# Gated attention and SwiGLU mix on one core: two gate-factor loads issued earlier, the first attention quad's fills dealt 4, 3, 3, and the last two PSUM banks swapped before some long visits

## The chip, the cores and the metric

One core of a Trainium2 chip runs the whole program in one launch. The metric is the device time of a launch in microseconds, and the number reported is the median over several launches. Beside it stands one launch that the hardware profiler recorded; its span runs from the first instruction to the last.

Engines are named as in the profile: PE multiplies matrices into PSUM, which has eight banks of 128 x 512 fp32; DVE, ACT and POOL work on vectors; SP issues DMA transfers, as ACT and POOL do too.

## The reference, cut to what matters

```python
x = A_x                                            # 1 x 2048 x 640
g = sigmoid((x * gate_w).sum(-1, keepdims=True))   # one gate factor per row
a = attention(x, wq, wk, wv, wo, beta)             # 32 heads of 20, 4 segments of 512
b = (silu(x @ w1) * (x @ w3)) @ w2                 # hidden width 1728
return g * a + (1 - g) * b
# attention, for each segment s of 512 rows and each head:
#   a_dot = softmax(q k^T * 20**-0.5 + causal mask) v
#   a_mem = phi(q) M / (phi(q) z + 1e-6)           # M, z from the segments before
#   o = sigmoid(beta) * a_mem + (1 - sigmoid(beta)) * a_dot
#   M += phi(k)^T v ; z += sum phi(k)
# the heads' outputs are joined and multiplied by wo
```

## The kernel before, in words

**Tiling.** The 2048 rows are four chunks of 512, one for each segment. Activations lie transposed, 128 features on the partitions and the 512 rows of a chunk along the free axis. Dense products split both operands into a high and a low part and make three passes (high by high, high by low, low by high). One output block of 128 x 512 that sums over 640 features is 15 matmuls into one PSUM bank.

**Dense work.** Q, K and V projections, the feed-forward network (`ffn_up` makes tiles named g and u, `ffn_down` makes tiles named f), the read of the memory from earlier segments (`memory_read`, tiles nd) and the output projection (`oproj`, tiles op) are generators. A generator yields after each few matmuls with an estimate of the PE time it has just laid down. Chunks 0 and 1 are group A, chunks 2 and 3 group B. The generators are strung together by hand into units; the list `segs` says up to which point of the attention each unit lasts.

**Attention.** The 128 pairs of a chunk and a head go through in 32 quads, four heads of one chunk at a time. Each quad owns 40 slots. At slot 5 (`BIG`) comes a long visit of PE to the attention, at slot 17 (`SMALL`) a short one. A visit deals fills from a table, `VISITS`: an `s` fill makes logits for the row maxima (two banks; DVE reduces them, L641), a `t` fill makes transposed logits of the quad before (two banks; ACT takes the exponential, L673), and `o` is the product with V (one bank; DVE copies it out, L691). A long visit has eight entries and takes 15 banks' worth of tiles, a short one three. For quad number m = 1 there is no `o` yet, and its long visit is split in two, at slots 5 and 11 (L800). Before a visit of fewer than four entries the dense work may stop in the middle of a block ("amid"); before one of four or more it runs on until no block is open ("between").

**Banks.** `bank_tile` (L111) takes PSUM banks round robin: it pops the first of the list `free`. A tile that is filled at once puts its bank at the end of the list straight away. A dense block that stays open for a while is `held`, and its bank goes to the end when the block is full (`filled`). Whoever writes a bank next must wait until the last reader of its old content is done.

**What sets the order.** PE's instructions stay in the order in which the program was written. The other engines' streams are laid out by a scheduler at build time, except for instructions marked `here`, which keep their place. All engines run their streams in order, so an instruction that waits holds up all that stands behind it on its engine.

**Gate factors.** The first row of `ed` in DRAM has, for each row of a chunk, the factor that the sum of both branches is multiplied by at the end. `load_share` (L738) broadcasts 512 of them to all 128 partitions, in a DMA issued from ACT's queue and marked `here`; the tile is called sh. `share` (L541) multiplies a finished output block by it: L543, on DVE, or on POOL for chunk 2 and the even blocks of chunk 1. Chunk 0's factors are loaded at the start of chunk 0's last down projection (L569), chunk 1's at the start of its output projection proper, behind the normalization (L831). Chunk 3 has a buffer of its own; chunks 0, 1 and 2 share one.

**Normalization.** `normalize` (L753) runs before a chunk's output projection, one block of 128 features at a time. A matmul spreads the softmax denominators (tile rr), and DVE multiplies the attention's output by them (L762). For chunks after the first, four transposes bring the memory's part (tile gt, L766), DVE adds it (L767), ACT rounds the sum to its high part (L768) and DVE takes the low part (L769). These blocks are braided into the up projections of a feed-forward unit, so PE works on a g or u block between them.

Of the kernel before, what the change touches and what calls it, by code (L numbers as in the profile page):

```python
# [25 lines left out]
BIG = -1.0e38  # L26
# [12 lines left out]
def gated_mix(ctx: ExitStack, tc: tile.TileContext, xT, wqk, wv, w13, w2, w2h, wo, beta, out):  # L39
# [63 lines left out]
    last = {}  # L103
# [5 lines left out]
    free, held = list(range(NB)), {}  # L109

    def bank_tile(name, hold=None):  # L111


        k = free.pop(0)
        ps = pp.tile([P, L], F32, tag=f"b{k}", name=name, bufs=1)
        if hold:
            held[k] = -hold
        else:
            free.append(k)
        return ps  # L120
# [443 lines left out]
    def ffn_down(cs, js, idx, last=()):  # L564
        first = js[0] == 0
        w2s = [w_get(i, idx[0]) for i in idx]
        for c in cs:
            if c in last and c < 2:
                load_share(c)  # L569
            if first:  # L570
                accs[c] = slot(f"acc{c}")[:, :KB * L].rearrange("p (b n) -> p b n", b=KB)
            for fb in range(KB):
                for n0, n1 in ((0, 256), (256, L)) if last and (c, fb) == (NSEG - 1, KB - 1) else ((0, L),):
                    ps = bank_tile(f"f{c}_{js[0]}_{fb}_{n0}", 1300 if len(js) > 2 else 690)
                    ms = []
                    for j, w in zip(js, w2s):
                        for a, b in (PASSES if j < NF else ((0, 0), (0, 1))):
                            ms.append((w[:, b, fb * P:(fb + 1) * P], hts[c, j][:, a, n0:n1]))
                    for n, (w, h) in enumerate(ms):
                        nc.tensor.matmul(ps[:, :n1 - n0], w, h, start=n == 0, stop=n == len(ms) - 1)  # L580
                        if n % 3 == 2 and n < len(ms) - 1:
                            yield 699.0 if n == 2 and len(ms) > 5 else 699
                    filled()
                    dst = accs[c][:, fb]
                    if first:
                        nc.scalar.copy(dst, ps)
                    elif c not in last:
                        nc.vector.tensor_add(dst, ps, dst)  # L588
                    elif c < 2:
                        finish(c, fb, ps)  # L590
                    else:
                        finish_shared(c, fb, ps, n0, n1 - n0)
                    yield 699 if len(ms) % 3 == 0 else 466

    def both_shares():
        for c in B:
            load_share(c)
            yield 1

# [153 lines left out]
    def normalize(c):  # L753

        assert c in turned
        if not c:
            gms[c] = big_tile(f"oT{c}", FR)[:, :KB * L].rearrange("p (b n) -> p b n", b=KB)
        for b in range(KB):
            o, hi = f_tile(f"on{c}_{b}"), gms[c][:, b]
            ps = bank_tile(f"rr{c}_{b}")  # L760
            nc.tensor.matmul(ps, sel[:, b * P:(b + 1) * P], rR, start=True, stop=True)
            nc.vector.tensor_mul(o, oall[c][:, b].bitcast(F32), ps)  # L762
            if c:
                pt = bank_tile(f"gt{c}_{b}")
                for qb in range(4):
                    nc.tensor.transpose(pt[:, qb * P:(qb + 1) * P], hi[:, qb * P:(qb + 1) * P].bitcast(F32), ident)  # L766
                nc.vector.tensor_add(o, o, pt)  # L767
            nc.scalar.copy(hi, o)  # L768
            nc.vector.tensor_sub(oall[c][:, b], o, hi.bitcast(F32))  # L769
            yield 700  # L770
# [22 lines left out]
    def attention():  # L793

        for m in range(-1, NQUAD + 2):
            for n in range(40):
                if m == -1 and n < 40 - LEAD:
                    continue

                todo = VISITS.get(n, ()) if m != 1 else {BIG: VISITS[BIG][:3], BIG + 6: VISITS[BIG][4:]}.get(n, VISITS.get(n, ()))  # L800
                todo = [(kind, m - q, f) for kind, q, *f in todo if 0 <= m - q < NQUAD]
                if todo:
                    yield "amid" if len(todo) < 4 else "between"
# [16 lines left out]
    def oproj(c, plan):  # L820

        ws, oT = [], []

        def first():
            yield from normalize(c)
            oT.extend((gms[c], oall[c]))

        def rest():
            ws.extend(w_get(i, plan[0]) for i in plan)
            if c == 1:  # L830
                load_share(c)  # L831
            for fb in range(KB):
                ps = bank_tile(f"op{c}_{fb}", 1300)
                n = 0
# [52 lines left out]
    def chain(jobs):  # L887
        return sum(c for c, _ in jobs), (y for _, g in jobs for y in g)
# [41 lines left out]
    seg = [d, braid(chain(u), o1, 5), o2] + [job_up(A, j) for j in GROUPS[3][2:]] + [job_down(A, 3)]  # L930
    u0, u1 = jobs_up_by_chunk(A, 4)
    x2, x3 = split_x(2), split_x(3)
    seg += [(0, load_raw(2)), (0, load_raw(3))] + u0 + [braid(chain(u1), (0, x2), 4, 0, False)]
    d = job_down(A, 4, (0,))
    q = job_q(B[:1], 0, {2: big_tile})
    seg += [braid(chain([braid(d, (0, x2), 5)] + q), (0, x3), 4, 10)] + job_v(B)
# [21 lines left out]
    segs.append((NJ + LAG, seg))  # L958
    d, u = job_down(B, 3), jobs_up(B, 4)
    o1, o2 = jobs_oproj(3)  # L960
    tail = [braid(chain([d, (0, both_shares())] + u), o1, 4, 10)] + [braid(o2, (0, shared(2)), 3), job_down(B, 4, B)]

    for n, (_, g) in enumerate(head):
        for _ in g:
# [29 lines left out]
    while run:  # L994
# [7 lines left out]
        if isinstance(place, str):  # L1002

            for _ in range(4 if place == "amid" else 8):
                if (max(held.values(), default=-1) >= 0) if place == "amid" else not held:
                    break
                d = step(run)
                if d is None:
                    break
                credit -= d  # L1010
            next(att)
        slots += 1
        credit += run[2]
# [66 lines left out]
```

## Time and profile before

| | |
|---|---|
| median of 3 launches | 1105.04 us (1104.69 to 1105.52) |
| the profiled launch | 1107.25 us |
| its span, first to last instruction | 1105.4 us |
| between that span and that launch's time | 1.85 us |
| the profiled launch above the median | 2.21 us |
| DVE busy | 598.1 us (54%) |
| POOL busy | 584.6 us (53%) |
| ACT busy | 381.3 us (34%) |

How to read it: a row of the timeline has the start in us from the start of the span, the time from the first of its instructions to the end of the last, engine, line, operation, written tile, read tiles, shape, and count. In brackets stands how long the engine was idle before it, and who released it. Matmuls are pipelined, so a 128 x 512 matmul is recorded for some 0.4 us though a new one starts every 0.23 us. A wait of PE therefore shows in brackets only as far as it outlasts the matmul before it; the whole of it is read from start times.

### The profile page before, as it was taken

Reading aid. Unit: us, or ns where it says so; the run is one execution under the profiler, and the core shown is the slowest. Engines: PE = TensorE matmul, PEld = TensorE weight load, DVE = VectorE, ACT = ScalarE, POOL = GpSimd, SP = SyncE. Lnnn points to the kernel's source line nnn. Section 1 sums busy time; section 2 is a strip of 40 time slices with the busy share of each in tenths; the row PEclk is TensorE's granted clock in tenths of the full one; section 3 lists DMA queues with packets and bytes.
Section 4 is the critical chain, followed back from the end, with each engine's and each line's share of the span. In section 5 each row is a group of like instructions: output and inputs, shape, how many; then the busy total and the mean of one; then the engine's idle time right before and its main releaser. Section 6 shows DMA issues by size and latency. Waiting matters only on the chain.

```text
span 1105.4 us, 17904 instructions
## 1 busy us (share of the span) xinstructions
PE 1094.9 (99%) x6290; PEld 853.0 (77%) x6290; DVE 598.1 (54%) x1711; ACT 381.3 (34%) x826; POOL 584.6 (53%) x729
## 2 busy tenths in 40 slices
PE   9999999999999999999999999999999999999998
PEld 6988877777777777787977777777777777777787
DVE  5032564356555554366153678875557665651575
ACT  6244233343233122145244543325333332223020
POOL 5055556366366363565066447556774665655263
PEclk9999999999999999999999999999999999999999
DMA  8256943334355134435367966365664343433122
GB/s 306 110 205 220 281 125 82 95 82 116 77 142 129 51 84 123 126 94 171 121 197 265 288 215 183 97 161 146 151 159 109 85 116 96 117 103 89 52 79 95
DMA packets 87545, 153.20 MB, mean 139 GB/s; under 512 B 11584, under 2 KB 25184, under 8 KB 87456
## 3 DMA queue, kind: packets, MB, share of 16 engines
q1 hardware_dynamic: 63040, 106.30, 30.1%
q0 software_dynamic: 20384, 38.68, 15.9%
q10 hardware_dynamic: 4032, 7.08, 1.8%
q8 instruction: 50, 0.82, 0.3%
q14 instruction: 39, 0.32, 0.1%
HBM read 96.56 MB, written 54.54 MB: 137 GB/s over the span
## 4 chain that ended last, share of the span: by engine, by line
PE 93%; DVE 4%; ACT 1%; DMA 1%; issue 1%; ACTq 0%; SPq 0%; DVEq 0%
PE g L257 16%; PE f L580 16%; PE u L257 16%; PE k L257 6%; PE v L385 6%; PE op L837 6%; PE o L687 6%; PE q L257 5%; PE s L634 5%; PE t L667 4%; PE nd L352 1%; PE pm L449 1%; PE q L327 1%; DVE junk L641 1%; DMA sh<-ed 1%
## 5 line engine op out<-in xcount | busy, mean ns | idle before, releaser
L641 DVE CUSTOM_DVE_ANT_0 junk<-s,mask 128x256 bf16<-128x256 f32 (+3 forms) x512 | 250.3, 489 | 105.9 <-PE s L634 73.6
L673 ACT ACTIVATE P<-t 128x512 f32<-128x512 f32 (+1 forms) x384 | 172.5, 536 | 190.2 <-PE t L667 153.0
L257 PE MATMUL g<-X,W 128*128 128x512 f32 x840 | 208.5, 398 | 0.0
L179 POOL TENSOR_TENSOR W<-wr,W 128x640 fp32r<-128x640 f32 (+1 forms) x126 | 198.5, 1581 | 2.5
L174 POOL CAST W<-wr 128x640 fp32r<-128x640 f32 (+1 forms) x126 | 92.5, 739 | 202.0 <-PE f L580 47.7
L580 PE MATMUL f<-ht,W 128*128 128x512 f32 (+1 forms) x825 | 197.0, 395 | 0.7 <-DVE acc L550 0.7
L257 PE MATMUL u<-X,W 128*128 128x512 f32 x780 | 196.7, 399 | 0.0
L677 POOL TENSOR_SCALAR_AFFINE_SELECT P<-P 128x256 f32<-128x256 f32 x192 | 94.6, 502 | 183.2 <-ACT P L673 182.9
L257 PEld LDWEIGHTS g<-X,W 128*128 128x128 f32 x840 | 155.9, 188 | 36.6 <-issue 0.4
L580 PEld LDWEIGHTS f<-ht,W 128*128 128x128 f32 x825 | 152.9, 188 | 37.6 <-DVE acc L550 1.5
L257 PEld LDWEIGHTS u<-X,W 128*128 128x128 f32 x780 | 144.0, 188 | 34.4 <-ACT P L673 0.3
L107 POOL TENSOR_TENSOR ht<-ft,ht 128x512 fp32r<-128x512 f32 x52 | 67.2, 1291 | 90.1 <-ACT ht L106 90.0
L611 POOL DMA_DIRECT2D qk<-qkd x128 | 83.6, 655 | 0.5 <-issue 0.2
L634 PE MATMUL s<-qk 60*128 60x256 f32 (+3 forms) x512 | 77.8, 345 | 1.1 <-DVE fu L520 1.0
L257 PE MATMUL k<-X,W 128*128 128x512 f32 x300 | 77.0, 403 | 0.0
L687 PE MATMUL o<-P,vg 128*32 128x512 f32 (+3 forms) x1024 | 75.5, 435 | 1.4 <-DVE on L767 1.4
L519 ACT ACTIVATE ft<-g 128x512 f32<-128x512 f32 x52 | 31.2, 599 | 124.9 <-PE g L257 113.8
L385 PE MATMUL v<-W,X 128*128 128x320 f32 (+1 forms) x480 | 71.9, 311 | 0.3 <-ACT P L673 0.3
L520 DVE SCALAR_TENSOR_TENSOR fu<-ft,g 128x512 f32<-128x512 f32 x52 | 35.7, 686 | 67.3 <-ACT ft L519 58.3
L385 PEld LDWEIGHTS v<-W,X 128*128 128x128 f32 x480 | 71.0, 189 | 1.0 <-ACT P L673 0.5
L106 ACT CAST ht<-ft 128x512 fp32r<-128x512 f32 x52 | 32.2, 619 | 110.9 <-DVE ft L528 110.8
L588 DVE TENSOR_TENSOR acc<-f,acc 128x512 f32<-128x512 f32 x65 | 44.7, 689 | 44.8 <-PE f L580 44.6
(123 smaller groups left out, 1204.8 us busy)
## 6 DMA issues: line engine op xcount, KB each, us to landing
qk<-qkd POOLq DMA_DIRECT2D x128, 240.0 KB, 4.0
wr<-in_w_dram SPq DMA_DIRECT2D x80, 320.0 KB
qkd<-qs SPq DMA_DIRECT2D x20, 512.0 KB
qkd<-ks SPq DMA_DIRECT2D x20, 512.0 KB
od<-oq SPq DMA_DIRECT2D x32, 256.0 KB
wr<-in_wo_dram SPq DMA_DIRECT2D x20, 320.0 KB
vg<-vd SPq DMA_DIRECT2D x16, 336.0 KB
xr<-in_xT_dram SPq DMA_DIRECT2D x20, 256.0 KB
```

The costliest lines, as they stand in the source:

```text
L107: (lo or nc.gpsimd.tensor_sub)(dst[:, 1], src, dst[:, 0].bitcast(F32))
L174: hi = nc.gpsimd.tensor_copy(w[:, 0, :n], raw[:, :n])
L179: last["low"] = nc.gpsimd.tensor_sub(w[:, 1, :n], raw[:, :n], w[:, 0, :n].bitcast(F32))
L257: nc.tensor.matmul(ps, w[:, a, kb * P:(kb + 1) * P], x[:, b, kb, :], start=n == 0, stop=n == 14)
L385: nc.tensor.matmul(ps[:, :n1 - n0], x[:, a, kb, lb * P:(lb + 1) * P], wvt[kb][:, b, n0:n1], start=n == 0, stop=n == 14)
L580: nc.tensor.matmul(ps[:, :n1 - n0], w, h, start=n == 0, stop=n == len(ms) - 1)
L611: here(nc.gpsimd.dma_start(t[64 * i:64 * i + RH], qkd[c][RH * (h + i):RH * (h + i + 1)]))
L634: nc.tensor.matmul(ps[i][:, o:o + w], q[:, qb * P:(qb + 1) * P], key[:, :w], start=n == 0, stop=n == len(todo) - 1, skip_group_check=True)
L641: nc.vector.tensor_tensor_reduce(out=junk[:, :w], in0=ps[i][:, o:o + w], in1=mask[:, L - w:], scale=1.0, scalar=-3.0e38, op0=ALU.add, op1= ...
L673: last["exp"] = nc.scalar.activation(pairs[2 * m + k]["P"][:, i, o:o + n], ps[i][:, b:b + n], AF.Exp, scale=SCALE)
L677: nc.gpsimd.affine_select(d, d, pattern=[[0, 2], [0, n], [1, P]], base=0, channel_multiplier=-1, compare_op=ALU.is_ge, fill=0.0)
L687: nc.tensor.matmul(ps[32 * i:32 * i + 32, kb * P:], heads[2 * p + i]["v"][:, kb], pairs[p + i // 2]["P"][:, i % 2, o:o + n], start=kb == 0 ...
```

## The change

Three edits that don't depend on each other.

1. **Loads of gate factors.** Chunk 0's load leaves `ffn_down` and is put among the loads of the raw inputs of chunks 2 and 3, ahead of the up projections of the last feed-forward group of chunks 0 and 1. Chunk 1's load moves from behind its normalization to ahead of it. The helper for chunks 2 and 3 takes a list and does what it did.
2. **First quad.** For m = 1 the long visit at slot 5 takes four fills in place of three (t fill 3 joins), and the one at slot 11 three in place of four. The short visit keeps three. With four, the first visit is now one of those before which no dense block stays open, and the second is one that may cut a block.
3. **Swap.** The last `held` dense tile's first letter and the bank of the last gt tile are remembered. Before a long visit, if the last but one bank in the list is that gt bank and the last dense tile was a u, f or o(p) block, the last two entries of the list change places.

```diff
@@ bank_tile
         if hold:
             held[k] = -hold
+            last["dense"] = name[0]
@@ ffn_down
         for c in cs:
-            if c in last and c < 2:
-                load_share(c)
             if first:
@@
-    def both_shares():
-        for c in B:
+    def load_shares(cs):
+        for c in cs:
             load_share(c)
             yield 1
@@ normalize
                 pt = bank_tile(f"gt{c}_{b}")
+                last["gt"] = free[-1]
@@ attention
-                todo = VISITS.get(n, ()) if m != 1 else {BIG: VISITS[BIG][:3], BIG + 6: VISITS[BIG][4:]}.get(n, VISITS.get(n, ()))
+                todo = VISITS.get(n, ()) if m != 1 else {BIG: VISITS[BIG][:3] + VISITS[BIG][4:5], BIG + 6: VISITS[BIG][5:]}.get(n, VISITS.get(n, ()))
@@ oproj
         def first():
+            if c == 1:
+                load_share(c)
             yield from normalize(c)
@@
         def rest():
             ws.extend(w_get(i, plan[0]) for i in plan)
-            if c == 1:
-                load_share(c)
@@ the units
-    seg += [(0, load_raw(2)), (0, load_raw(3))] + u0 + [braid(chain(u1), (0, x2), 4, 0, False)]
+    seg += [(0, load_raw(2)), (0, load_raw(3)), (0, load_shares(A[:1]))] + u0 + [braid(chain(u1), (0, x2), 4, 0, False)]
...
-    tail = [braid(chain([d, (0, both_shares())] + u), o1, 4, 10)] + [braid(o2, (0, shared(2)), 3), job_down(B, 4, B)]
+    tail = [braid(chain([d, (0, load_shares(B))] + u), o1, 4, 10)] + [braid(o2, (0, shared(2)), 3), job_down(B, 4, B)]
@@ the loop over slots, before a visit
+            if place == "between" and free[-2] == last.get("gt") and last["dense"] in "ufo":
+                free[-2:] = free[:-3:-1]
             next(att)
```

In the rows that follow, a name's first digits are chunk, quad or block, and its last number is only a serial number. Line numbers are those of each kernel.

**PE in the first quad.** Before, from the last matmuls of the memory read nd1_2_0 (chunk 1) to the second visit:

```order
L634 MATMUL s1_0_1_1476<-qk1_91 128x512
L667 MATMUL t0_0_0_1483<-qk0_90 128x512
L667 MATMUL t0_1_1_1492<-qk0_90 128x128
L257 MATMUL u1_0_1438<-X1_105,W16_989 128x512 x3
L257 MATMUL g0_1_1507<-X0_103,W17_1075 128x512 x6
L352 MATMUL nd1_2_1_1520<-Ms0_4_1145,pq1_271 128x147
L257 MATMUL g0_1_1507<-X0_103,W17_1075 128x512 x9
L667 MATMUL t0_3_0_1543<-qk0_90 128x512
L634 MATMUL s1_2_0_1551<-qk1_91 128x512
L634 MATMUL s1_1_1_1571<-qk1_91 128x128
L352 MATMUL nd1_3_0_1589<-Ms0_0_714,pq1_271 128x147
```

Now:

```order
L258 MATMUL u1_0_1438<-X1_105,W16_989 128x512 x3
L633 MATMUL s1_0_1_1483<-qk1_91 128x512
L666 MATMUL t0_1_1_1499<-qk0_90 128x128
L666 MATMUL t0_3_1_1508<-qk0_90 128x512
L258 MATMUL g0_1_1515<-X0_103,W17_1075 128x512 x6
L353 MATMUL nd1_2_1_1528<-Ms0_4_1145,pq1_271 128x147
L633 MATMUL s1_2_0_1536<-qk1_91 128x512
L633 MATMUL s1_1_1_1556<-qk1_91 128x128
L258 MATMUL g0_1_1515<-X0_103,W17_1075 128x512 x9
L353 MATMUL nd1_3_0_1589<-Ms0_0_714,pq1_271 128x147
```

The last three matmuls of u1_0 moved ahead of the first visit, t0_3 from the second visit to the first, and the second visit now cuts the open block g0_1 after six of its matmuls in place of following it. The matmuls are the same. With the round robin this changes which old content each tile waits for: g0_1 now takes the bank of s1_0_0 (before, that of nd1_2_0), t0_3_1 that of u1_0, and s1_1_1 that of t0_3_1 (before, that of g0_1).

**DVE at chunk 0's last down projection.** f0_13_n and f1_13_n are its output blocks of chunks 0 and 1, X2 and X3 the low parts of the inputs of chunks 2 and 3. Before:

```order
L550 TENSOR_TENSOR acc0_1953<-f0_13_1_0_5020,acc0_1953 128x512
L132 TENSOR_TENSOR X2_4932<-xr2_4776,xh2_3_5038 128x512
L550 TENSOR_TENSOR acc0_1953<-f0_13_2_0_5029,acc0_1953 128x512
L543 TENSOR_TENSOR acc0_1953<-acc0_1953,sh0_4999 128x512 x2
L550 TENSOR_TENSOR acc0_1953<-f0_13_3_0_5047,acc0_1953 128x512
L132 TENSOR_TENSOR X2_4932<-xr2_4776,xh2_4_5065 128x512
L543 TENSOR_TENSOR acc0_1953<-acc0_1953,sh0_4999 128x512
L550 TENSOR_TENSOR acc0_1953<-f0_13_4_0_5056,acc0_1953 128x512
```

Now:

```order
L551 TENSOR_TENSOR acc0_1953<-f0_13_1_0_5020,acc0_1953 128x512
L544 TENSOR_TENSOR acc0_1953<-acc0_1953,sh0_4790 128x512 x2
L133 TENSOR_TENSOR X2_4934<-xr2_4776,xh2_3_5038 128x512
L551 TENSOR_TENSOR acc0_1953<-f0_13_2_0_5029,acc0_1953 128x512
L133 TENSOR_TENSOR X2_4934<-xr2_4776,xh2_4_5065 128x512
L551 TENSOR_TENSOR acc0_1953<-f0_13_3_0_5047,acc0_1953 128x512
L551 TENSOR_TENSOR acc0_1953<-f0_13_4_0_5056,acc0_1953 128x512
L544 TENSOR_TENSOR acc0_1953<-acc0_1953,sh0_4790 128x512
```

The first two multiplications by the gate factors stand right behind the add of block 1 in place of block 2. From there to the add of the last block, f1_13_4, DVE has 19 instructions in both kernels. On ACT, the load of sh0 stands directly behind the last exponential of the visit before the g blocks, some twenty instructions earlier than it did; on SP, the store of the first finished block now stands ahead of one weight load.

**ACT and DVE at the normalization of chunk 1.** on1_b is the block being normalized, u2_2 the dense block around it, s19, t18 and o34 the fills of the visit that follows. ACT before:

```order
L655 DMA qk0_90<-mr_7222 2x8x128 x2
L768 CAST gm1_6764<-on1_0_7250 128x512
L519 ACTIVATE ft2_2_7269<-g2_2_7233 128x512
L768 CAST gm1_6764<-on1_1_7277 128x512
L673 ACTIVATE P36_7326<-t18_0_0_7324 128x512
L106 CAST ht2_2_7268<-ft2_2_7269 128x512
```

ACT now:

```order
L654 DMA qk0_90<-mr_7222 2x8x128 x2
L739 DMA sh1_7250<-ed1_85 128x512
L768 CAST gm1_6764<-on1_0_7252 128x512
L520 ACTIVATE ft2_2_7271<-g2_2_7233 128x512
L768 CAST gm1_6764<-on1_1_7279 128x512
L672 ACTIVATE P36_7328<-t18_0_0_7326 128x512
```

DVE before:

```order
L762 TENSOR_TENSOR on1_1_7277<-oall1_6264,rr1_1_7278 128x512
L767 TENSOR_TENSOR on1_1_7277<-on1_1_7277,gt1_1_7281 128x512
L762 TENSOR_TENSOR on1_2_7298<-oall1_6264,rr1_2_7299 128x512
L528 SCALAR_TENSOR_TENSOR ft2_2_7269<-fu2_2_7270,u2_2_7273 128x512
L641 ISA junk_7320,m76_7138<-s19_0_0_7316,mask_89 128x512
L767 TENSOR_TENSOR on1_2_7298<-on1_2_7298,gt1_2_7302 128x512
L769 TENSOR_TENSOR oall1_6264<-on1_1_7277,gm1_6764 128x512
```

DVE now:

```order
L761 TENSOR_TENSOR on1_1_7279<-oall1_6264,rr1_1_7280 128x512
L761 TENSOR_TENSOR on1_2_7300<-oall1_6264,rr1_2_7301 128x512
L767 TENSOR_TENSOR on1_1_7279<-on1_1_7279,gt1_1_7283 128x512
L767 TENSOR_TENSOR on1_2_7300<-on1_2_7300,gt1_2_7304 128x512
L529 SCALAR_TENSOR_TENSOR ft2_2_7271<-fu2_2_7272,u2_2_7275 128x512
L640 ISA junk_7322,m76_7138<-s19_0_0_7318,mask_89 128x512
L769 TENSOR_TENSOR oall1_6264<-on1_1_7279,gm1_6764 128x512
```

The load of chunk 1's factors now stands ahead of the cast of on1_0. The add of gt1_2 moved from behind the first reduction of s19 to ahead of the read of u2_2. Swapped are the banks that o34 and t18_3_0 take: o34 now follows u2_2, t18_3_0 follows gt1_2. The rule fires at one more visit, some 65 us later and without a normalization beside it: there o40 takes the bank of f3_0_1 and t21_3_0 that of f3_0_0, the other way round than before. No other tile changes the content that it waits for, but for those of the first quad.

## The prediction

> **What bounds the kernel now.** I read the page first, then PE's waits, then the timelines around the waits. On the page:
>
> ```profile
> PE 1094.9 (99%) x6290; PEld 853.0 (77%) x6290; DVE 598.1 (54%) x1711; ACT 381.3 (34%) x826; POOL 584.6 (53%) x729
> PE 93%; DVE 4%; ACT 1%; DMA 1%; issue 1%; ACTq 0%; SPq 0%; DVEq 0%
> ```
>
> PE is the bound nearly everywhere: it is busy for 99% of the span and holds 93% of the chain that ended last. All that can be won without fewer matmuls is where PE waits. One long stretch of the chain gives PE's pace, and the list of PE's waits the longest ones:
>
> ```profile
> 354.61 21.00 PE f L580 x90
> ...
> PE o L687 <- DVE on L767: 1.4, 1, 1.4
> PE s L634 <- DVE fu L520: 1.0, 1, 1.0
> PE f L580 <- DVE acc L550: 0.7, 2, 0.4
> ```
>
> A 128 x 512 matmul every 0.233 us; and but for the start of the program no wait exceeds 1.4 us. The three edits go one to each of these rows. So some 5 us, 0.45%, is the most that can come of it, and the question is how much of each wait is replaced by another. I call the three places A (first quad), B (chunk 0's last down projection) and C (normalization of chunk 1).
>
> **A: the first quad.** PE, DVE and ACT there:
>
> ```profile
> 145.60 0.85 PE L352 MATMUL nd<-Ms,pq 128*128 128x147 f32 x6
> 146.38 0.50 PE L634 MATMUL s<-qk 60*128 60x512 f32 x2
> 147.27 0.97 PE L257 MATMUL u<-X,W 128*128 128x512 f32 x3
> 148.22 1.64 PE L257 MATMUL g<-X,W 128*128 128x512 f32 x6
> 153.41 0.33 PE L634 MATMUL s<-qk 60*128 60x384 f32 x1
> 154.72 0.50 PE L634 MATMUL s<-qk 60*128 60x384 f32 x3 [0.98 <-DVE fu L520]
> ...
> 146.69 0.25 DVE L358 RECIPROCAL nd_r<-nd_r 128x16 f32<-128x16 f32 x1
> 147.52 0.55 DVE L359 SCALAR_TENSOR_TENSOR gm<-nd,gate,nd_r 128x320 f32<-128x320 f32 x1
> 148.59 0.68 DVE L528 SCALAR_TENSOR_TENSOR ft<-fu,u 128x512 f32<-128x512 f32 x1
> ...
> 147.14 2.07 ACT L673 ACTIVATE P<-t 128x512 f32<-128x512 f32 x4 [4.01 <-PE t L667]
> ```
>
> The last s fill wants the bank of g0_1, whose matmuls end just ahead of the visit; ACT and DVE have yet to read it. The two halves of the fill start 1.31 apart, of which 0.98 is idle; I count 1.1 as wait. Before that, three u matmuls take 0.95 in place of 0.70; 0.1 of it is the change from the visit's small tiles, so 0.14 is wait. **Removed: 1.24.**
>
> What comes in: g0_1 now takes s1_0_0's bank. The three u matmuls go first, so the visit starts at 146.38 + 0.70 = 147.08. Its first three fills took 0.89 (146.38 to 147.27), t0_3 another 0.34 (the s pair of 512 columns in B's rows, 512.34 to 512.68), and g0_1 could start at 148.31. DVE is free at 146.94, and in its new order makes gm (0.55), ft1_0 (0.68) and then the reduction of s1_0_0 (0.69 for this size); each starts some 0.07 before the one ahead ends, so the bank is free at 146.95 + 0.48 + 0.61 + 0.69 = 148.73, and g0_1 starts near 148.8. **Added: 0.49.** The second visit's last fill now waits for the exponential of t0_3_1, the seventh ACT instruction in a row. The first starts 0.76 behind the visit, at 147.84, and they follow every 0.48 ((2.07 - 0.62) / 3), so the seventh ends at 151.3. The fill comes near 151.5 (148.8, six g matmuls 1.40, six nd matmuls 0.78, then s and t fills of 0.34 and 0.24): just in time. Behind it nothing is late: g0_1's reader is next wanted in the short visit, over 2 us on. **A gains 1.24 - 0.49 = 0.75.** Bounds: 1.24, if g0_1 doesn't wait, and -0.1, if both ACT and DVE run half a microsecond later than reckoned and PE waits for each.
>
> **B: the gate factors of chunk 0.**
>
> ```profile
> 502.30 2.47 PE L580 MATMUL f<-ht,W 128*128 128x512 f32 x10
> 505.07 1.44 PE L580 MATMUL f<-ht,W 128*128 128x512 f32 x5 [0.30 <-DVE acc L550]
> 508.67 3.74 PE L257 MATMUL q<-X,W 128*128 128x512 f32 x15 [0.36 <-DVE acc L588]
> 512.34 0.51 PE L634 MATMUL s<-qk 60*128 60x512 f32 x2
> 512.68 1.28 PE L667 MATMUL t<-qk 62*128 62x512 f32 x6
> 513.89 1.06 PE L687 MATMUL o<-P,vg 128*32 128x512 f32 x8
> ...
> 497.89 0.69 DVE L550 TENSOR_TENSOR acc<-f,acc 128x512 f32<-128x512 f32 x1 [0.36 <-PE f L580]
> 503.12 1.29 DVE L543 TENSOR_TENSOR acc<-acc,sh 128x512 f32<-128x512 f32 x2 [3.35 <-DMA sh<-ed]
> 512.12 1.28 DVE L588 TENSOR_TENSOR acc<-f,acc 128x512 f32<-128x512 f32 x2
> ...
> 496.37 0.32 ACTq L740 DMA_DIRECT2D sh<-ed  x1
> ```
>
> The load is issued at 496.37, DVE wants it at 503.12 - 3.35 = 499.77 and gets it at 503.1. Then DVE works off its backlog without a break, 15 instructions from 503.12 to 512.12, one per 0.60, up to the add of f1_13_4, which ends at 513.40. PE pays: twenty f matmuls from 502.30 should bring q at 506.96; it starts at 508.67, **1.71** late. In the visit behind it, the six t matmuls take 1.21 up to o. In A's first visit, where nothing waited, the same six took 0.55 (147.27 - 146.38, less 0.34 for the s pair). That is **0.66** more.
>
> With the load ahead of six blocks (6 x 15 x 0.233 = 21 us earlier) and at most 6.7 us long, DVE never waits for it. That cover would have to shrink by two thirds before it cost anything. The issue itself, 0.32 on ACT, falls where ACT stands idle behind a visit's exponentials: nothing. On SP the first store now stands ahead of a weight load and waits for DVE, so that load goes some 3 us later; its tile isn't split before the W slot is free, after the f blocks, and that hides it.
>
> So DVE decides. From the add at 497.89 to f1_13_4's add it has 19 instructions; at 0.60 the last starts at 509.3 and ends at 510.0, and PE, unhindered, would want it near 511.2 (the visit 1.71 earlier, at 510.63, then 0.34 and one t pair of 0.23). That would give back all of 2.37. But the first two multiplications move into a time when POOL is at work:
>
> ```profile
> 498.30 0.72 POOL L174 CAST W<-wr 128x642 fp32r<-128x642 f32 x1
> 499.11 1.58 POOL L179 TENSOR_TENSOR W<-wr,W 128x642 fp32r<-128x642 f32 x1
> 507.66 0.93 POOL L174 CAST W<-wr 128x642 fp32r<-128x642 f32 x1 [6.97 <-PE f L580]
> ...
> 703.28 1.28 POOL L107 TENSOR_TENSOR ht<-ft,ht 128x512 fp32r<-128x512 f32 x1 [5.75 <-ACT ht L106]
> 703.45 1.66 DVE L769 TENSOR_TENSOR oall<-on,gm 128x512 fp32r<-128x512 f32 x1
> ```
>
> The last two rows give the price. A DVE instruction with two SBUF inputs that starts inside a POOL instruction ends 0.55 after POOL does (703.28 + 1.28 = 704.56; 703.45 + 1.66 = 705.11); alone it takes 0.69. The multiplications are of this kind, the adds (one input in PSUM) are not. The first, from 498.49, meets the cast that ends at 499.02 and ends at 499.57 in place of 499.18. POOL's subtraction, due at 499.11, has waited by then; it goes next, with its remaining 1.44, to 501.01. The second multiplication ends at 501.56 in place of 499.78. The chain is late by 1.78, and f1_13_4's add ends at 511.75 against 513.40. **B gains 1.65**; a wait of about 0.6 stays in the visit. Bounds: 2.37 without the collision, and 0.9 if two later multiplications meet POOL's next casts too (0.4 each).
>
> The Trainium skill, page "SBUF — State Buffer", section "Who interferes with whom", speaks against the edit in the same way: a DVE instruction with two SBUF inputs and a POOL instruction that reads SBUF exclude each other, and whoever starts first keeps the port for the whole instruction. By that rule B gives 1.65; if both engines could share, 2.37. The trace agrees with the rule (0.55 us behind POOL's end, above).
>
> **C: the normalization.**
>
> ```profile
> 703.68 2.36 PE L687 MATMUL o<-P,vg 128*32 128x512 f32 x32 [1.38 <-DVE on L767]
> ...
> 696.52 1.07 ACTq L655 DMA_DIRECT2D qk<-mr  x2
> 697.79 0.62 ACT L768 CAST gm<-on 128x512 fp32r<-128x512 f32 x1 [2.85 <-DMA qk<-mr]
> ...
> 698.45 0.69 DVE L769 TENSOR_TENSOR oall<-on,gm 128x512 fp32r<-128x512 f32 x1 [1.24 <-ACT gm L768]
> 702.85 0.68 DVE L767 TENSOR_TENSOR on<-on,gt 128x512 f32<-128x512 f32 x1
> 706.24 0.68 DVE L691 COPY oq<-o 128x512 f32<-128x512 f32 x1
> ```
>
> Now o34 waits for the add of gt1_2, which ends at 703.53, and starts 0.15 later. The whole chain hangs on ACT's cast at 697.79, which stands idle behind two DMA issues until 697.59. The moved load of sh1 is a third issue there: 0.32 and a step of 0.04, so the cast and DVE's 698.45 come 0.36 later. DVE then runs its new order: the sub at 698.81, fu2_2, two multiplies, two adds, and ft2_2 as the seventh, from 698.81 + 6 x 0.60 = 702.41 to 703.09. o34, on u2_2's bank, starts at 703.24: 0.44 earlier. The last s fill of the visit waits for the copy of o34, which before came at 706.24 because DVE was behind. It needs o34's end (703.24 + 2.36) and two reductions and two subs on DVE from 703.0 on, with at most 0.2 lost to POOL, since POOL's ht2_2, the culprit at 703.28, now stands behind the selects of P36: copy near 705.7. **C gains 0.5.** Bounds: 1.5 if all waits go, and -0.8 if ht2_2's 1.28 gets in ahead of the second sub and the copy ends near 707.7. If sh1's issue were not here, the gain would be 0.36 more; behind the normalization, where it was, the load met no wait.
>
> The swap that fires once more, at o40, costs nothing:
>
> ```profile
> 767.36 0.59 ACT L586 COPY acc<-f 128x512 f32<-128x512 f32 x1 [1.51 <-PE f L580]
> 768.14 2.36 PE L687 MATMUL o<-P,vg 128*32 128x512 f32 x32
> ```
>
> The copy that reads f3_0_1 ends at 767.95, and with the 0.15 of above o40 could start at 768.10. If ACT did an exponential first, it would cost 0.5.
>
> **Sum.** 0.75 + 1.65 + 0.5 = 2.9. The profiled span of 1105.4 becomes 1102.5, and that launch's 1107.25 becomes 1104.35. The launches shown have a median of 1105.04, 2.21 below the profiled one; from there the forecast is **1102.1**.
>
> **Rivals.** (1) *The collisions cost less*: POOL's instructions fall between DVE's, and all waits but small ones go: 2.37 + 1.1 + 1.2 = 4.7, 1100.3. For it: a collision hangs on tenths; against it: the cast at 498.30 is there in both kernels. (2) *A and C only swap waits*: DVE and ACT run as full as before in both, only B pays: 1105.04 - 1.65 = 1103.4. For it: C's DVE is busy without a break from 698.45 on, and A's two new waits are near. (3) *Slower: the multiplications run into POOL*. Place B. Before, POOL stood idle for 6.97 until 507.66, and four of five multiplications fell where it did nothing. Each that meets a 1.58 subtraction costs 1.4. The last add would end at 510.0 + 1.4 n against 513.40: from n = 2.5 on B loses, and with A and C's 1.25 counted, the kernel is slower from n = 3.4, so four; with all five the add ends at 517.0 and the time is 1105.04 + 3.6 - 1.25 = 1107.4. Against it: POOL's next split waits for PE's f blocks, and only one subtraction lies in reach. (4) *The load isn't earlier*: ACT reaches it late, or it waits on the queue for the input loads ahead of it, and DVE still waits. Then A and C alone count: 1103.8. Against it: 21 us of room.
>
> **How the numbers follow.** Forecast 0.57, rival 1 0.14, rival 2 0.19, rival 3 0.05, rival 4 0.05. The bound of 0.2% (2.2 us, about what a measurement can tell from no change) lies at 1102.8, within reach of the forecast's own range of 1101.4 to 1103.0: of its 0.57 some 0.5 lies below, and with rival 1 that is 0.64 faster. The rest of the forecast with rivals 2 and 4 is 0.31 within the bound, rival 3 0.05 slower. The range takes in rivals 2 and 4 and half of rival 1: 1100.8 to 1104.0.
>
> **What would show it.** A: s no longer waits for fu; g waits some 0.4 for a reduction. B: no DVE wait for sh; the f and q waits gone; two multiplications near 499 at 1.1 and 2.1 in place of 0.7, and t12_1_0 still waiting half a microsecond for f1_13_4's add. C: o waits for ft2_2 some 0.9; the cast starts near 698.15. Wrong: if a wait of over a microsecond stands anywhere near these places, or one in the second half of the program that wasn't there.

## The result and the profile after

| | before | now |
|---|---|---|
| median, 20 launches each | 1104.99 us (1104.17 to 1107.23) | 1103.70 us (1102.75 to 1105.05) |
| profiled launch | 1107.25 us | 1103.47 us |
| its span | 1105.4 us | 1101.8 us |

The medians differ by 1.29 us (0.12%); the ratio is 0.9985, 95% interval 0.9979 to 0.9991. That is faster, but inside the 0.2% that counts as no change. The prediction was 1102.1 us; the measured median is 1.6 above it and inside the stated range.

The spans of the two profiles differ by 3.65 us, nearly three times as much as the medians. The sections below show why. First the profile after: the chain of the page, and the head of PE's list of waits.

```profile
PE 95%; DVE 3%; ACT 1%; issue 1%; DMA 0%; SPq 0%; DVEq 0%
```
```profile
PE warm L915 <- DVE zero L912: 1.3, 1, 1.3
PE o L686 <- DVE ft L529: 0.7, 1, 0.7
PE v L386 <- ACT P L672: 0.3, 1, 0.3
```

The waits of s for fu, of f and q for acc and of o for on are gone from the list. In their place stands one new wait, o for ft, of 0.7. The chain holds 95% PE in place of 93%.

**Place A**, the timeline of PE in the first quad after, then of DVE there:

```profile
144.97 0.85 PE L353 MATMUL nd<-Ms,pq 128*128 128x147 f32 x6
146.47 0.50 PE L633 MATMUL s<-qk 60*128 60x512 f32 x2
148.17 1.68 PE L258 MATMUL g<-X,W 128*128 128x512 f32 x6
150.50 0.50 PE L633 MATMUL s<-qk 60*128 60x512 f32 x2
151.08 0.41 PE L633 MATMUL s<-qk 60*128 60x384 f32 x4
151.42 2.38 PE L258 MATMUL g<-X,W 128*128 128x512 f32 x9
153.63 0.85 PE L353 MATMUL nd<-Ms,pq 128*128 128x147 f32 x6
154.27 0.94 PE L258 MATMUL u<-X,W 128*128 128x512 f32 x3
...
147.42 0.68 DVE L640 CUSTOM_DVE_ANT_0 junk<-s,mask 128x512 bf16<-128x512 f32 x1
```

This launch was 0.62 ahead of the profiled one of before when it came here, so 0.62 is added for the comparison. The visit starts at 147.09 (predicted 147.08) and g0_1 at 148.79 (predicted 148.8), 0.07 behind the end of the reduction of s1_0_0 (without the shift 148.17 against 147.42 + 0.68 = 148.10). The last s fill, in two halves 1.31 apart before, is now one row of 0.41. In before's timeline the second visit and the end of the stretch stood here:

```profile
152.60 0.50 PE L667 MATMUL t<-qk 62*128 62x512 f32 x2
155.16 0.95 PE L352 MATMUL nd<-Ms,pq 128*128 128x147 f32 x6
155.90 1.41 PE L257 MATMUL u<-X,W 128*128 128x512 f32 x5
```

The second visit took 155.16 - 152.60 = 2.56 and now 151.42 - 150.50 = 0.92; without the t0_3 pair, which moved out of it (0.34), that is 1.30 less. From nd1_2_0 to the u block PE took 155.90 - 145.60 = 10.30 and now takes 154.27 - 144.97 = 9.30: **A gained 1.00.**

**Place B**, PE, DVE, POOL and ACT's queue after:

```profile
505.40 3.63 PE L258 MATMUL q<-X,W 128*128 128x512 f32 x15
509.30 1.48 PE L666 MATMUL t<-qk 62*128 62x512 f32 x6
510.71 2.36 PE L686 MATMUL o<-P,vg 128*32 128x512 f32 x32
...
496.38 0.69 DVE L551 TENSOR_TENSOR acc<-f,acc 128x512 f32<-128x512 f32 x1 [0.36 <-PE f L579]
496.99 3.05 DVE L544 TENSOR_TENSOR acc<-acc,sh 128x512 f32<-128x512 f32 x2
508.94 1.28 DVE L587 TENSOR_TENSOR acc<-f,acc 128x512 f32<-128x512 f32 x2
...
496.79 0.72 POOL L175 CAST W<-wr 128x642 fp32r<-128x642 f32 x1
497.59 1.91 POOL L180 TENSOR_TENSOR W<-wr,W 128x642 fp32r<-128x642 f32 x1
...
469.42 0.33 ACTq L739 DMA_DIRECT2D sh<-ed  x1
```

The load is issued 27 us ahead of its use, and DVE no longer waits for it. Instead the two multiplications take 3.05 (alone 1.29): the first is held by POOL's cast, POOL's subtraction by the first (1.91 in place of 1.58), the second by the subtraction. The last add, f1_13_4's, ends at 508.94 + 1.28 = 510.22, which is 511.73 with the 1.51 that this launch was ahead; predicted 511.75. PE pays only in the visit, where the six t matmuls take 1.41 up to o.

**Place C**, PE, DVE, ACT and POOL after:

```profile
700.22 2.36 PE L686 MATMUL o<-P,vg 128*32 128x512 f32 x32 [0.70 <-DVE ft L529]
...
699.39 0.68 DVE L529 SCALAR_TENSOR_TENSOR ft<-fu,u 128x512 f32<-128x512 f32 x1
701.81 0.69 DVE L769 TENSOR_TENSOR oall<-on,gm 128x512 fp32r<-128x512 f32 x1
702.64 0.69 DVE L690 COPY oq<-o 128x512 f32<-128x512 f32 x1
...
695.14 0.62 ACT L768 CAST gm<-on 128x512 fp32r<-128x512 f32 x1 [3.31 <-DMA qk<-mr]
...
702.75 1.29 POOL L107 TENSOR_TENSOR ht<-ft,ht 128x512 fp32r<-128x512 f32 x1
```

Shifted by the 3.11 that this launch was ahead, the cast stands at 698.25 (predicted 698.15), o34 at 703.33 (703.24), the copy at 705.75 (705.7). DVE's subtraction takes 0.69 in place of 1.66, since POOL's ht2_2 comes behind it.

### The profile page after: what moved, and what is told of

Its sections match the earlier page's. It is cut to its first block, busy times and chain, and to the rows that moved or that the text cites. A ratio compares the mean times of both kernels' runs of the same rounds, so it can differ in the third digit from the quotient of the medians.

```text
span 1101.8 us, 17903 instructions
## 1 busy us (share of the span) xinstructions
PE 1094.2 (99%) x6290; PEld 853.8 (77%) x6290; DVE 599.1 (54%) x1711; ACT 381.1 (35%) x826; POOL 584.1 (53%) x729
## 4 chain that ended last, share of the span: by engine, by line
PE 95%; DVE 3%; ACT 1%; issue 1%; DMA 0%; SPq 0%; DVEq 0%
PE g L258 18%; PE u L258 17%; PE f L579 17%; PE v L386 7%; PE k L258 6%; PE op L837 6%; PE o L686 6%; PE q L258 5%; PE s L633 5%; PE t L666 4%; PE nd L353 1%; PE pm L450 1%; PE q L328 1%; DVE junk L640 1%; PE gt L766 1%; PE pkt L435 1%
```

## The experiments

The first row is the comparison above. The others were timed in rounds against before in three sessions, in which before had a median of 1105.28 us (before again, only A, B and C), 1105.20 (A and C, swap alone, the two kernels with other multiplications) and 1105.58 (sh1 alone, no swap, change again). In the last four columns stands what the profiled launch of each kernel gained (-) or lost against the profiled launch of before, from the start times of the first matmul of a block before and behind each place: the program's start up to block u1_0 (142 us), A from there to u0_2 (176), B from u1_12 (492) to v2_0_1 (520), C from g2_2 (692) to u3_2 (712).

| kernel | median us | ratio (95%) | start | A | B | C |
|---|---|---|---|---|---|---|
| change, first profile | 1103.70 | 0.9985 (0.9979 to 0.9991) | -0.62 | -1.00 | -1.67 | -0.49 |
| change, again | 1103.99 | 0.9984 (0.9975 to 0.9993) | +0.05 | -1.00 | -1.67 | -0.49 |
| before, again | 1105.03 | 1.0000 (0.9991 to 1.0009) | -0.68 | -0.01 | **-2.15** | 0.00 |
| only A | 1104.23 | 0.9992 (0.9983 to 1.0001) | -0.15 | -1.02 | **-2.13** | +0.23 |
| only B | 1105.60 | 1.0003 (0.9994 to 1.0012) | +1.51 | 0.00 | -1.67 | -0.01 |
| only C | 1104.86 | 0.9993 (0.9984 to 1.0002) | -0.27 | 0.00 | **-0.55** | -0.51 |
| A and C | 1104.14 | 0.9989 (0.9980 to 0.9999) | +0.42 | -1.02 | **-1.79** | -0.49 |
| swap alone | 1105.08 | 1.0002 (0.9993 to 1.0011) | -0.29 | 0.00 | **-1.82** | +0.01 |
| sh1 alone | 1104.72 | 0.9989 (0.9979 to 1.0000) | +1.33 | 0.00 | **-2.21** | -0.72 |
| change, two multiplications on POOL | 1103.34 | 0.9987 (0.9977 to 0.9996) | -0.25 | -1.00 | -2.25 | -0.49 |
| change, three multiplications later | 1103.59 | 0.9987 (0.9978 to 0.9996) | +0.01 | -1.06 | -2.25 | -0.48 |
| no swap, two multiplications on POOL | 1103.50 | 0.9981 (0.9972 to 0.9990) | +3.12 | -1.02 | -2.25 | -0.70 |

The numbers in bold come from kernels that do not touch place B at all. Only A's +0.23 at C, which it does not touch either, comes with DVE's add of gt1_1, which waits 0.46 for PE's gt matmuls in that launch and 0.10 in before's. Why it does was not settled, and C is therefore not read from one launch alone.

**Before, again** (no edit).

> The kernel before, unchanged, profiled a second time. Two theories on why the medians differ by 1.29 us where the two profiles differ by 3.65. Theory 1, the launch: the first profiled launch of before (1107.25) was slow at the program's start and elsewhere, and a usual one pays the same waits at the three places (DVE 3.35 for sh, PE 1.0 for fu, PE 1.4 for on). Then a launch near 1105.0 shows a DVE wait for sh of 3.0 to 3.7. Theory 2, the wait: in a usual launch the load of sh0 lands one to two microseconds earlier, and B had less to win than the profile showed. Then a launch near 1105.0 shows a DVE wait for sh of under 2.3, and PE starts q at under 508.0 minus the difference at the start of the program. Either way the time is that of before: ratio 1.000 within 0.001.

Its profiled launch took 1104.26 us. DVE's row for the first multiplications:

```profile
500.35 1.29 DVE L543 TENSOR_TENSOR acc<-acc,sh 128x512 f32<-128x512 f32 x2 [1.21 <-DMA sh<-ed]
```

The load was issued at 495.74 and used 4.61 later; in the first profile it took 6.75 (496.37 to 503.12). The wait is 1.21 in place of 3.35, and the PE of an unchanged kernel is 2.15 faster at B. Theory 2 holds.

**Only A, only B, only C.** Only A (the part of the line that changes):

```diff
-{BIG: VISITS[BIG][:3], BIG + 6: VISITS[BIG][4:]}
+{BIG: VISITS[BIG][:3] + VISITS[BIG][4:5], BIG + 6: VISITS[BIG][5:]}
```

> Only the first quad dealt 4, 3, 3. Theory 1 (each place is worth what the two profiles differ by, in every launch): -0.9 us, ratio 0.9992. Rival (the gain of A is an accident of the one profile): 0.0 within 0.3. In the profile either way: PE waits for no fu in the first quad, and g0_1 starts 0.3 to 0.6 behind t0_3.

Only B (the helper that takes a list is left out):

```diff
-            if c in last and c < 2:
-                load_share(c)
-    seg += [(0, load_raw(2)), (0, load_raw(3))] + u0 + [...]
+    seg += [(0, load_raw(2)), (0, load_raw(3)), (0, load_shares(A[:1]))] + u0 + [...]
```

> Only chunk 0's gate factors loaded a unit ahead. Theory 1 (the profile's wait for sh is paid in every launch): -1.6 us, ratio 0.9986. Theory 2 (the load lands earlier in a usual launch): 0.0 to -0.6 us. In the profile either way: no DVE wait for sh, two multiplications near 499 that take 1.1 and 2.1, f1_13_4's add later than DVE's work alone would have it, and t12_1_0 waiting about half a microsecond.

Only C (the two lines that set `last["dense"]` and `last["gt"]` are left out here):

```diff
         def first():
+            if c == 1:
+                load_share(c)
             yield from normalize(c)
...
-            if c == 1:
-                load_share(c)
...
+            if place == "between" and free[-2] == last.get("gt") and last["dense"] in "ufo":
+                free[-2:] = free[:-3:-1]
```

> Only the swap of the last two banks and chunk 1's gate factors loaded ahead of its normalization. Theory 1: -0.5 us, ratio 0.9995. Rival (the swap gains 0.85 and the load's issue on ACT takes 0.36 of it back): the same here, told apart by the swap alone. Rival (o34 only swaps one wait for another, and what it gains is lost by the end): 0.0 within 0.3.

The differences of the medians are -1.05, +0.32 and -0.42 us, -1.15 together; the whole change has -1.29. Each ratio's interval is about as wide as these differences and takes in 1, so the times alone show no gain for any of them; but only B's interval, 0.9994 to 1.0012, leaves out the 0.9986 of theory 1. Its +0.32 is also outside the 0.0 to -0.6 of theory 2, which priced the wait and not the collision that comes in its place. The profiles put A and C where theory 1 has them (but for only A's +0.23 at C), and B where theory 2 has it. The profile of only C shows the wait of B in an intermediate size:

```profile
502.32 1.29 DVE L544 TENSOR_TENSOR acc<-acc,sh 128x512 f32<-128x512 f32 x2 [2.77 <-DMA sh<-ed]
```

Over the seven profiles with B untouched DVE's wait for sh was 3.35, 2.77, 1.51, 1.51, 1.23, 1.21 and 1.13. Against the kernels where nothing waits at B any more (-2.25), PE lost 2.25, 1.70, 0.46, 0.43, 0.12, 0.10 and 0.04 there: each time the wait less 1.1. So DVE has 1.1 to spare at this place, and of a usual wait of 1.5 PE feels 0.4.

**A and C, without B** (the edits of only A and only C).

> The change without its move of chunk 0's gate factors: the first quad dealt 4, 3, 3, the swap, and chunk 1's factors ahead of the normalization. If the load of sh0 lands some 4.6 after its issue in a usual launch (theory 2), the move of sh0 is worth nothing or costs up to 0.4, and this kernel stands where the whole change stands: ratio 0.9984 to 0.9988. If the wait of 3.35 is the usual one (theory 1), it stands 1.6 us above the whole change: ratio 0.9999. In the profile: sh waited for by DVE for 1.0 to 1.5 by theory 2, 3.0 to 3.7 by theory 1.

DVE waited 1.51 for sh, at the edge of theory 2's 1.0 to 1.5 and far from theory 1's 3.0 to 3.7. The ratio, 0.9989, is 0.0001 above theory 2's range and 0.0010 below theory 1's. The median is 1.06 below before, the change's own 1.29 and 1.59 in its two comparisons; the ratio's interval holds those of the change. The move of sh0 is worth little either way.

**Multiplications kept off POOL's split.** Two kernels, each the whole change with one more edit. First, two multiplications on POOL:

```diff
-        i = (nc.gpsimd if c == 2 or c == 1 and fb % 2 == 0 else nc.vector).tensor_mul(d, d, shares[c])
+        i = (nc.gpsimd if c == 2 or c == 1 and fb % 2 == 0 or c == 0 and fb < 2 else nc.vector).tensor_mul(d, d, shares[c])
```

> The whole change, with the multiplications of chunk 0's first two blocks by its gate factors on POOL in place of DVE. They stand ahead of the split that collided with them, and DVE has two instructions fewer. If the collision of DVE's multiplications with POOL's cast and subtraction is what was left of the waits at B, they go: f1_13_3, f1_13_4 and q2_0 wait for nothing, t12_0 follows at pace, and PE gains 0.6 to 0.8 against the whole change there. If something else holds the adds up, PE starts t12_0 where it did. Ratio 0.9980 to 0.9983 against 0.9985.

Second, the multiplications of the first three blocks behind the add of block 3 (`behind` holds that add and `owed` the blocks that still have to be multiplied, both empty at first; the dependency only fixes the order on DVE; its further arguments are left out):

```diff
+        if c == 0 and fb < 2:
+            tc.add_manual_dep(i.ins, behind[0].ins.name, ...)
...
-        nc.vector.tensor_add(d, ps, d)
-        share(c, fb)
-        nc.sync.dma_start(out[c, fb], d)
+        added = nc.vector.tensor_add(d, ps, d)
+        owed.append((c, fb))
+        if fb == 3:
+            behind[:] = [added]
+        while owed and (c or fb >= 3):
+            e = owed.pop(0)
+            share(*e)
+            nc.sync.dma_start(out[e[0], e[1]], accs[e[0]][:, e[1]])
```

> The whole change, with the multiplications of chunk 0's first three blocks held on DVE until the add of block 3, when POOL has finished its split. DVE's work is the same, the collision is gone: each multiplication takes 0.6 a piece. If the collision alone holds the adds up, PE gains 0.6 to 0.8 at B against the whole change, as with the multiplications on POOL. If DVE's plain amount of work there is the limit, PE gains under 0.3. Ratio 0.9980 to 0.9985.

The three multiplications of the second kernel on DVE, in one row; then PE's visit with the two on POOL, up to the t pair behind o:

```profile
499.92 1.88 DVE L544 TENSOR_TENSOR acc<-acc,sh 128x512 f32<-128x512 f32 x3
```
```profile
509.60 0.63 PE L666 MATMUL t<-qk 62*128 62x512 f32 x6
510.16 2.36 PE L686 MATMUL o<-P,vg 128*32 128x512 f32 x32
512.72 0.50 PE L666 MATMUL t<-qk 62*128 62x512 f32 x2 [0.20 <-DVE pq L292]
```

Three multiplications in 1.88 is 0.6 a piece, and the six t matmuls take 0.56 up to o in place of 1.41. Both kernels gain 0.58 at B against the change, by the same amount though only the first takes work from DVE, and there nothing waits for an add any more: the collision alone had held them up. (In the first, one later multiplication still met POOL's cast and took 1.18; that is within DVE's slack.) Not all of the visit's 0.85 (1.41 - 0.56) is kept: the t pair behind o now waits for pq and starts 2.56 behind o, where it was 2.29 in the change, so 0.27 goes back. Since DVE has 1.1 to spare, the collision's 1.78 should leave 0.68; it left 0.58. In the times it doesn't show: ratios of 0.9987 for both, where 0.9980 to 0.9985 was expected.

**Swap alone** (the lines with `last["dense"]`, `last["gt"]` and the swap).

> Only the swap of the last two banks; chunk 1's gate factors stay behind the normalization. If the load's issue in front of ACT's cast takes 0.36 of C's gain, as the prediction has it, C is 0.7 to 0.9 here where swap and load together were 0.48 by the profiles: the cast of on1_0 follows the second qk issue without a third, and o34 starts 0.36 earlier against the steps before it. If the load costs nothing, C is 0.4 to 0.5 here too. Ratio 0.9991 to 0.9997.

C gained nothing, where 0.7 to 0.9 was expected. PE, then DVE and POOL of this kernel:

```profile
700.39 2.36 PE L688 MATMUL o<-P,vg 128*32 128x512 f32 x32 [0.17 <-DVE ft L529]
703.70 0.57 PE L635 MATMUL s<-qk 60*128 60x512 f32 x2 [0.51 <-DVE m L642]
704.90 0.50 PE L635 MATMUL s<-qk 60*128 60x384 f32 x3 [0.29 <-DVE oq L692]
...
701.37 1.67 DVE L771 TENSOR_TENSOR oall<-on,gm 128x512 fp32r<-128x512 f32 x1
...
701.20 1.29 POOL L107 TENSOR_TENSOR ht<-ft,ht 128x512 fp32r<-128x512 f32 x1 [5.76 <-ACT ht L106]
```

o34 does start 1.2 earlier against the steps around it. But POOL's ht2_2 still meets DVE's subtraction (1.67), the second reduction and the copy stand behind that, and the next two s fills wait for them until everything is given back. The streams of ACT, DVE and POOL are in before's order here; the new order, in which ht2_2 comes later, is not the swap's doing.

**sh1 alone** (the load moved, no swap).

> Only chunk 1's gate factors loaded ahead of its normalization, without the swap. The swap alone gave back what it gained, since POOL's ht2_2 still met DVE's subtraction. Theory: the moved load is what re-lays ACT's, POOL's and DVE's streams, and C's gain comes from there; then it comes here without the swap too: o34 waits for gt1_2's add, DVE's subtractions take 0.69 each, the copy of o34 comes 0.6 to 0.8 after o34's last matmul, and PE gains 0.4 to 0.8 at C. Rival: both edits are needed, o34 waits here as long as before (1.4), and C gains under 0.2. Ratio 0.9993 to 0.9997 by the theory, 0.9999 or more by the rival.

PE, DVE and POOL of this kernel:

```profile
701.85 2.36 PE L687 MATMUL o<-P,vg 128*32 128x512 f32 x32
704.95 0.93 PE L634 MATMUL s<-qk 60*128 60x384 f32 x4
...
702.83 0.69 DVE L769 TENSOR_TENSOR oall<-on,gm 128x512 fp32r<-128x512 f32 x1
704.64 0.68 DVE L691 COPY oq<-o 128x512 f32<-128x512 f32 x1
...
704.98 1.28 POOL L107 TENSOR_TENSOR ht<-ft,ht 128x512 fp32r<-128x512 f32 x1
```

With the load in front of the cast, the build lays ht2_2's cast behind the exponentials of P36, POOL's ht2_2 comes 2.15 behind the subtraction's start, and C gains 0.72. The swap on top of it costs 0.23, since it lets o34 wait for ft2_2 (0.70 in the change) where gt1_2's add is done 0.6 sooner. That rests on more than one launch: the six that have load and swap gain 0.48 to 0.51 at C, the two that have the load alone 0.72 and 0.70 (the second is below). The theory holds by the profile; the ratio, 0.9989, is below the 0.9993 to 0.9997 expected, with an interval that takes these in.

**No swap, two multiplications on POOL** (the change without its swap, and with chunk 0's first two multiplications on POOL as above).

> The whole change without the swap, and with the multiplications of chunk 0's first two blocks on POOL. If the swap is worth nothing beside the moved load of sh1, this stands 0 to 0.3 us below the whole change with those multiplications on POOL; if the swap is needed, 0.3 to 0.5 above it. Ratio 0.9984 to 0.9988; median 1103.0 to 1103.6 where before is 1105.2. Against the unchanged change in the same session: 0.4 to 0.8 us below by the profiles.

A, B and C together gain 3.97 by its profile, the change 3.16. Its median is 0.49 below that of the change in the same session (1103.50 and 1103.99), within the 0.4 to 0.8 expected, and its ratio, 0.9981, is below the 0.9984 to 0.9988 expected; but the intervals of the two ratios overlap: it is the best of the versions by its steps, and not shown to be faster by its times. Its profiled launch also shows what a start can cost, 3.12 us more than that of before. Below, the first matmuls, and the windows from 5 to 15 us (busy us of PE, PEld, DVE, ACT and POOL, granted PE clock, DMA share, GB/s):

```profile
8.12 8.15 PE L327 MATMUL q<-X,W 128*128 128x512 f32 x22 [1.37 <-ACT W L106]
```
```profile
5.00:10.00 5.00, 3.16 (x8) 1.89 (x9) 3.10 (x5) 2.70 (x5) 0.73 (x1) 0.74 1.04 387
10.00:15.00 5.00, 5.00 (x15) 3.91 (x14) 4.31 (x6) 3.77 (x6) 3.15 (x3) 0.58 1.01 338
```

The granted clock was 0.74 and 0.58 there, and the 22 matmuls took 0.37 each; in before's launch it was 1.00 in both windows.

**The change, again.**

> The changed kernel, unaltered, a second time. If a usual launch gains A 0.9, C 0.5 and nothing at B, the ratio is 0.9985 to 0.9990 and PE's steps at the three places repeat those of its first profile within 0.2. If the gain of the first comparison was an accident of that session, the ratio is over 0.9993.

Ratio and steps repeat: A -1.00, B -1.67, C -0.49 to the hundredth in two launches whose starts lie 0.67 apart.

## Why the prediction was right and where it failed

**The result's direction and bounds were right, the size was over twice too large** (2.9 against 1.29), and the likeliest class, faster by over 0.2%, did not come. The 1103.70 lies outside the forecast's own range, 1101.4 to 1103.0. It is inside the stated one because that was widened for rivals 2 and 4, neither of which came about, so that part is luck.

- **A** was 0.75 and measured 1.00. The visit's start and g0_1's wait came at the hundredth where reckoned. What was removed was mis-sized: the wait of the last s fill, counted as 1.1 from the gap between its two halves, was 1.30 by the length of the whole visit. The 0.05 that is left is spread over the tiles around.
- **B** was 1.65 and measured 1.67 against the launch that it was reckoned from. The collision, its size and the end of the last add were right; the wait left in the visit is 0.85 in place of about 0.6, since the visit came 0.16 sooner than reckoned. And the rule of the Trainium skill that the prediction cites ("SBUF — State Buffer", section "Who interferes with whom") is borne out: the two multiplications took 3.05 in POOL's way in place of 1.29, and out of its way 0.58 more was won, twice. The bound without collision, 2.37, measured 2.25, since the t pair behind o then waits for pq.
- **C** was 0.5 and measured 0.49, and o34 and the copy came within 0.1 of the forecast. One sentence of it fell: "If sh1's issue were not here, the gain would be 0.36 more". Without it the gain was zero, because the moved load, not the swap, gives the order in which POOL's ht2_2 misses DVE's subtraction. I had read the new order as the change's and not asked which of its two edits made it. The swap, which the gain was put down to, cost 0.23; the sum came out because it was worked out from the order that both edits make together.
- **The sum** of the three, 2.9, is 3.16 by the profiles (1.00 + 1.67 + 0.49). With the start of the program, 0.62, which the change doesn't touch, and 0.13 lost in small steps elsewhere, that is the 3.65 between the two spans.
- **The step that failed** is the last of the sum: "The launches shown have a median of 1105.04, 2.21 below the profiled one; from there the forecast is 1102.1". It takes 2.9 off the median as well. But the 2.21 were not a constant beside the kernel: they were in good part the wait at B. The profiled launch had the longest of seven waits for sh, 3.35; five of the other six were 1.5 or less, of which PE feels 0.04 to 0.46, and the change's collision costs it 0.58. So B is worth -1.67 in the launch that was profiled and, as an estimate, about +0.1 in a usual one. A usual launch gains 1.00 + 0.49 - 0.1 = 1.4, and 1.29 was measured. The waits of launches without a profile can't be seen; that they are like those five is argued, and the ratio of only B, 1.0003, fits it.
- Of the rivals none came true as told. "Only B pays" (1103.4) had it the wrong way round. The fourth (1103.8) came nearest, with A and C alone, but for another reason: the load is early, and what it saves is small and taken back by the collision.

## What to carry to other kernels

A profile is one launch. Where the wait to be removed ends with a DMA, and where the profiled launch stands above the median, find out first how long that wait is in other launches; a saving must not be taken off a median that has never paid it. A wait also costs PE only what it exceeds the waiting engine's slack (here 1.1 us), and an edit that removes it can bring a smaller cost that is paid in every launch.

When a list scheduler lays out the streams, ask of each new order which of the edits causes it: at place C an edit meant for a load's timing re-laid three engines and made the whole gain, and the one meant for the banks took a third of it back.

## What the runs showed of the hardware

- The same 256 KB broadcast load, issued at the same place of the program, was used 4.5 to 6.75 us after its issue over seven profiled launches, with DVE idle until it came. The bytes are not what differs most. Before DVE's release at 503.12 in the first profile of before, and at 500.35 in the second, the DMA engines show this (windows view: busy us of the engines, PE clock, DMA share, GB/s; the first profile, then the second):

```profile
500.37:501.37 1.00, 1.00 (x6) 0.80 (x5) 0.00 (x0) 0.97 (x3) 0.32 (x1) 1.00 0.17 59
501.37:502.37 1.00, 1.00 (x6) 0.82 (x5) 0.00 (x0) 0.83 (x2) 0.00 (x0) 1.00 0.00 0
502.37:503.12 0.75, 0.75 (x5) 0.62 (x4) 0.00 (x0) 0.00 (x0) 0.00 (x0) 1.00 0.00 0
```
```profile
499.24:500.24 1.00, 1.00 (x6) 0.83 (x5) 0.00 (x0) 0.98 (x2) 0.80 (x1) 1.00 0.19 63
500.24:500.35 0.11, 0.11 (x2) 0.07 (x2) 0.00 (x0) 0.11 (x1) 0.00 (x0) 1.00 0.00 0
```

  This view counts a packet whole in the window in which it starts. In the first profile, next to nothing starts in the last 1.75 us and DVE still waits (1.18 in the launch of only C, from 501.14 to 502.32); in the second it is 0.1. The DMA view of the first profile for 500.9:503.12 shows what is left (packets, MB, share of 16 engines):

```profile
q8 instruction: 1, 0.02, 2.6%
q10 hardware_dynamic: 1, 0.00, 0.1%
```

  q10 is the queue of this load. By the trace's records of packets and semaphores, the load ends with 16 packets of 4 bytes, each followed by one step of the semaphore that DVE waits for. Fifteen of them start by 500.88 and their steps come 0.30 to 0.37 later. The last one starts at 501.93, at the end of a 16 KB packet of instructions (501.01 to 501.95), and its step comes 1.10 later, at 503.03. Only C's launch shows the same: fifteen by 500.53, the last at 501.13, at the end of an instruction packet (500.20 to 501.14), its step 1.10 later. In the other five launches the load's last packet does not come at the end of an instruction packet. Without what the last packet lost (1.05 + 0.76, and 0.60 + 0.76), the waits of 3.35 and 2.77 would be 1.5 and 1.4, like the others. That the instruction packet is the cause is not shown: no run moved it.
- The program's start differs by 3.8 us between profiled launches (-0.68 to +3.12 in the table), more than all three edits are worth. The two latest starts go with a lower granted clock from 5 to 15 us: 0.74 and 0.58 in no swap (+3.12), 0.84 and 0.81 in only B (+1.51); in the other eleven launches it was 1.00. sh1 alone (+1.33) waits for its first weights and inputs instead. What lowered the clock is not shown.
- Where no wait ends with a DMA, launches mostly repeat to a few hundredths of a microsecond: with the load moved, B is -1.67 in three launches and -2.25 in three others. Only A's +0.23 at C is the exception.
